# Convolution of batch 1 on 64-by-32 tiles, with its shifted copies made by GpSimd and inside SBUF, batch 2's loads moved behind them, and W2 of group 3 a slot sooner

## The chip, the cores and the metric

One core of a Trainium2 chip. The time is device time of one execution in microseconds (us). A program on one core has no second core to compare clocks with, so each run is listed with the clock that TensorE (PE) was granted. PE does matmuls; VectorE (DVE) and ScalarE (ACT) take results out of PSUM (the kernel's pool there has eight buffers); GpSimd (POOL) makes copies in SBUF and issues the loads of x, which cast from float32 to bf16; SyncE (SP) issues stores, transposes by DMA and, in the changed kernel, three copies inside SBUF.

## The reference, cut to what matters

```python
def _attn_ref(x, weight):              # x: 8 x 4224 x 192, weight: 8 heads x 7 taps
    w = softmax(weight)                # per head
    out = einsum('hk,bskhg->bshg', w, x_unf)      # causal convolution of 7 taps along s

def _moe_ref(x, U, V, w_ch1, w_ch2):   # x: the convolution's result y
    h = x.transpose(0, 2, 1) @ U @ V   # rank 32, sums over all of s of one batch
    u = x + h.transpose(0, 2, 1)
    return u + relu(u @ w_ch1) @ w_ch2
```

The sum over s (`tt` below) needs a batch's whole convolution before the first u of that batch. The 264 tiles of 128 rows are worked off as 33 groups of 8: W1 (u times w_ch1), relu, W2 (times w_ch2), store.

## The kernel before: the parts that matter

```python
    def x_part(b, r, s0, s1):               # one of four loads of a batch, cast to bf16
        blk = NB0 * r + s0 - 1
        return nc.gpsimd.dma_start(out=xt[b][HB * r : HB * r + HB, s0:s1, :], in_=...)

    def x_shift(b):                         # the shifted copy of x for 64-by-32 tiles, 6 steps
        xbt[b] = xbs.tile([P, NB1, D], BF16, name="xb_sb")      # one buffer
        ...
        return [same(0, m), same(m, NB0, (NB0, NB1)),           # 128 partitions each
                ahead(0, 0, m), ahead(0, m, NB0), ahead(1, 0, m), ahead(1, m, NB1)]  # 32 each

    def conv32(b, h0, nh, engs): ...        # 64-by-32 tiles, 8 matmuls a head, needs xbt[b]
    def conv(b, h0, nh, rs, engs, ...): ... # 64-by-64 tiles, 8 matmuls a head, needs only xt[b]

    # a slot: W1 of some groups; W2 of some groups in blocks; what is done ahead of which block
    SLOTS = [
        ([0], [], {}),
        ([1], [0], {0: ["h0"], 1: ["h3", "l2:2"], 2: ["l2:3"]}),           # l: a load
        ([2], [1], {0: ["d1", "h1"], 1: ["t1"], 3: ["s1"], 4: ["h4", "x2:6"]}),
        ([3], [2], {1: ["h5"], 3: ["h6"]}),
        ([4, 5], [3, 4, 5], {0: ["h7"], 2: ["c2:0:3:AAD"], ..., 4: ["c2:6:2:A", "x3:4"], ...}),
    ]
    # d: conv of a batch, and the transpose of group 3 held back until it is over
    # c: conv32; x2:6: six steps of x_shift(2); t, s: sum over s; h: u of a group, then transpose

    # loads of batch b, held until matmuls of W1 of (group, m) are done; each pops one open x_shift step
    LOADS = {2: [(1, 5), (1, 5)], 3: [(4, 1), (4, 4), (5, 1), (5, 4)]}
    for b in range(4, B):
        g = 3 * b - 6
        LOADS[b] = [(g, 0), (g, 3), (g + 1, 0), (g + 1, 3)]
```

## Time and profile before

| kernel before | |
|---|---|
| median (6 runs, lowest to highest) | 325.21 us (325.11 to 325.31) |
| span of the profiled run, granted clock | 323.5 us, 1.0 |
| PE, DVE, ACT, POOL busy | 98%, 83%, 53%, 44% |
| batch 2's loads: first issue, last landing | 29.4, 44.9 us |
| batch 3's loads: first issue, last landing | 60.0, 73.1 us |
| batch 3's convolution starts | 95.1 us |

Four lines of GpSimd's timeline (start, length, engine, line, operation, and in brackets the idle time before it with its releaser):

```profile
42.52 5.43 POOL L293 COPY xb_sb<-x_sb 128x3072 bf16<-128x3072 bf16 x2 [8.89 <-DMA x_sb<-in_x_dram]
...
59.98 1.63 POOL L79 DMA_DIRECT2D x_sb<-in_x_dram  x2
...
71.39 5.43 POOL L293 COPY xb_sb<-x_sb 128x3072 bf16<-128x3072 bf16 x2 [6.20 <-PE ps L339]
...
87.52 3.08 POOL L305 COPY xb_sb<-x_sb 32x3456 bf16<-32x3456 bf16 x1
```

GpSimd alternates: the copies of batch 2 wait for its loads (42.5), the loads of batch 3 are issued only when those copies are over (60.0), and the copies of batch 3 wait for PE's convolution of batch 2 (71.4), because the shifted copy has one buffer. So in the kernel before the loads of batch 3 are there in time, though with only 1.0 us to spare (the last landed at 73.1, its copy began at 74.1), and PE is the releaser. The copies are over at 90.6, 4.5 us before PE wants them.

### The profile page before, as it was taken

What the parts mean: (1) busy time and instruction counts of PE and PEld (TensorE: products, weight loads), DVE (VectorE), ACT (ScalarE), POOL (GpSimd) and SP (SyncE); (2) the same over time, 40 slices, a digit from 0 to 9 for tenths busy, and PEclk for the clock granted to TensorE, in tenths of its full rate; (3) what the DMA queues carried; (4) which work ended last, traced back from release to release, by engine and by line L of the source; (5) the groups of instructions that cost most, each with busy time, mean ns of one, the idle gap of its engine ahead of it and who ended that gap; (6) DMA issues with size and microseconds to landing.
All of it is one profiled execution on the core that took longest, in us unless ns stands there. A gap on an engine that the chain in (4) does not pass through costs nothing.

```text
span 323.5 us, 9584 instructions
## 1 busy us (share of the span) xinstructions
PE 317.1 (98%) x3996; PEld 223.2 (69%) x3996; DVE 269.1 (83%) x551; ACT 170.4 (53%) x344; POOL 142.7 (44%) x111
## 2 busy tenths in 40 slices
PE   6999999999999999999999999999999999999996
PEld 3757676478677647866864784587797497487495
DVE  6769989987977986998798699879898897896864
ACT  1766624860874397088339708824903902912920
POOL 8664179729947694786859497000000000000000
PEclk9999999999999999999999999999999999999999
DMA  8999993999996899699699976139269059048035
GB/s 104 192 192 178 209 211 99 203 195 248 210 153 180 229 175 169 170 162 195 166 238 183 192 162 181 33 112 244 58 168 267 8 149 268 25 121 271 2 119 176
DMA packets 122907, 53.52 MB, mean 165 GB/s; under 512 B 87760, under 2 KB 122832, under 8 KB 122864
## 3 DMA queue, kind: packets, MB, share of 16 engines
q1 hardware_dynamic: 84528, 38.08, 47.0%
q0 software_dynamic: 38192, 14.73, 39.6%
q8 instruction: 31, 0.51, 0.7%
q14 instruction: 12, 0.10, 0.1%
q10 hardware_dynamic: 144, 0.10, 0.1%
HBM read 29.49 MB, written 25.95 MB: 171 GB/s over the span
## 4 chain that ended last, share of the span: by engine, by line
PE 92%; ACT 3%; DMA 2%; DVE 1%; issue 0%; POOL 0%; POOLq 0%
PE ps L583 42%; PE ps L554 39%; PE ps L339 3%; PE ps L457 3%; DMA x_sb<-in_x_dram 2%; PE ps L402 2%; ACT rl_sb L568 2%; PE ps L369 1%; ACT y_sb L256 1%; PE ps L509 1%; DVE u_sb L479 1%; DVE rl_sb L570 1%; PE ps L524 0%; PE ps L428 0%; POOL x_sb L79 0%
## 5 line engine op out<-in xcount | busy, mean ns | idle before, releaser
L568 ACT ACTIVATE rl_sb<-ps 128x512 bf16<-128x512 f32 x233 | 124.3, 603 | 108.0 <-PE ps L554 96.0
L583 PE MATMUL ps<-W_sb,rl_sb 128*128 128x192 bf16 x1584 | 141.9, 246 | 0.2
L583 PEld LDWEIGHTS <-rl_sb 128*128 128x128 bf16 x1584 | 128.1, 98 | 13.5 <-issue 13.1
L554 PE MATMUL ps<-uT,W_sb 64*128 64x512 bf16 x1188 | 131.7, 376 | 0.0
L570 DVE TENSOR_SCALAR rl_sb<-ps 128x512 bf16<-128x512 f32 x163 | 105.3, 688 | 15.7 <-PE ps L554 15.4
L554 PEld LDWEIGHTS <-W_sb 64*128 64x128 bf16 x1188 | 66.9, 94 | 60.5 <-issue 3.9
L592 DVE TENSOR_TENSOR out_sb<-ps,u_sb 128x384 f32<-128x384 f32 (+1 forms) x133 | 70.4, 550 | 25.9 <-PE ps L583 25.4
L305 POOL COPY xb_sb<-x_sb 32x3072 bf16<-32x3072 bf16 (+1 forms) x24 | 67.6, 2826 | 0.7
L479 DVE TENSOR_TENSOR u_sb<-y_sb,ps 128x192 bf16<-128x192 bf16 (+1 forms) x168 | 66.3, 461 | 0.0
L293 POOL COPY xb_sb<-x_sb 128x3072 bf16<-128x3072 bf16 x12 | 32.6, 2744 | 34.6 <-PE ps L339 25.7
L256 ACT ACTIVATE y_sb<-ps 128x384 bf16<-128x384 f32 (+4 forms) x90 | 38.2, 514 | 10.7 <-PE ps L339 7.9
L79 POOL DMA_DIRECT2D x_sb<-in_x_dram x32 | 27.1, 849 | 17.5 <-PE ps L554 10.5
L258 DVE CAST y_sb<-ps 128x408 bf16<-128x408 f32 (+4 forms) x36 | 19.2, 578 | 1.1 <-PE ps L369 0.9
L457 PE MATMUL ps<-tt_sb,V_sb 32*128 32x192 bf16 x264 | 12.4, 246 | 0.1
L339 PE MATMUL ps<-xb_sb,band 64*32 64x384 bf16 x192 | 12.1, 332 | 0.0
L339 PE MATMUL ps<-x_sb,band 64*32 64x384 bf16 x192 | 12.1, 333 | 0.0
L457 PEld LDWEIGHTS <-V_sb 32*128 32x128 bf16 x264 | 4.7, 92 | 7.3 <-issue 7.3
L416 ACT ACTIVATE tt_hi<-ps 128x192 bf16<-128x192 f32 x8 | 2.6, 331 | 10.9 <-PE ps L402 10.9
L369 PE MATMUL ps<-x_sb,band 64*64 64x240 bf16 (+3 forms) x192 | 8.1, 276 | 0.3 <-DMA x_sb<-in_x_dram 0.3
L369 PEld LDWEIGHTS <-band 64*64 64x64 bf16 x192 | 6.0, 106 | 2.2 <-issue 1.5
L339 PEld LDWEIGHTS <-band 64*32 64x32 bf16 x384 | 4.5, 89 | 4.1 <-issue 3.0
L402 PE MATMUL ps<-y_sb,U_sb 128*32 128x192 bf16 x258 | 7.4, 247 | 0.0
(65 smaller groups left out, 69.0 us busy)
## 6 DMA issues: line engine op xcount, KB each, us to landing
out_dram<-out_sb SPq DMA_DIRECT2D x131, 192.0 KB, 2.7
x_sb<-in_x_dram POOLq DMA_DIRECT2D x14, 384.0 KB, 7.3
x_sb<-in_x_dram POOLq DMA_DIRECT2D x7, 432.0 KB, 7.3
x_sb<-in_x_dram POOLq DMA_DIRECT2D x7, 408.0 KB, 8.0
x_sb<-in_x_dram POOLq DMA_DIRECT2D x1, 504.0 KB, 7.6
uT<-u_sb SPq DMA_TRANSPOSE x31, 3.9
x_sb<-in_x_dram POOLq DMA_DIRECT2D x1, 480.0 KB, 5.9
W_sb<-in_moe_w_ch_dram POOLq DMA_DIRECT2D x2, 192.0 KB, 7.6
```

Source lines behind the costliest of these rows:

```text
L79: return nc.gpsimd.dma_start(out=xt[b][HB * r : HB * r + HB, s0:s1, :], in_=x[b, blk * HB : (blk + s1 - s0) * HB, :].rearrange("(j p) d -> ...
L256: nc.scalar.activation(out=out, in_=in_, func=ACT.Copy)
L293: nc.gpsimd.tensor_copy(out=xbt[b][:, s0:s1, :], in_=xt[b][:, s0 + 1 : s1 + 1, :])
L305: nc.gpsimd.tensor_copy(out=xbt[b][q, s0:s1, :], in_=xt[b][q, s0:s1, :])
L339: nc.tensor.matmul(out=pp[r][QB * cg : QB * cg + QB, 0 : nk[r] * GS], lhsT=w[hr], rhs=t[hr, st : st + 2 * nk[r] - 1 : 2, hs], start=True, ...
L457: nc.tensor.matmul(out=banks[pr][:, a * D : (a + 1) * D], lhsT=V_sb[32 * q : 32 * q + 32, (j // 8) * 2 + j % 2, :], rhs=ttb[b][32 * q : 32 ...
L479: nc.vector.tensor_tensor(out=u_group(g)[:, i : i + n, :, hf, :], in0=yt[b][:, run[0] : run[0] + n, :].rearrange("p n (c k) -> p n c k", c=3),
L554: last = nc.tensor.matmul(out=pps[m][hf][:], lhsT=W1_sb[HB * hf : HB * hf + HB, c, m * P : (m + 1) * P], rhs=uTt[g][HB * hf : HB * hf + HB ...
L568: nc.scalar.activation(out=rl[:, m, hf, :], in_=pp[hf][:], func=ACT.Relu)
L570: nc.vector.tensor_scalar_max(out=rl[:, m, hf, :], in0=pp[hf][:], scalar1=0.0)
L583: last = nc.tensor.matmul(out=cps[:, a * D : (a + 1) * D], lhsT=rlt[g][:, m, hf, (i + a) * P : (i + a + 1) * P], rhs=W2_sb[:, m, :], start ...
L592: nc.vector.tensor_tensor(out=o[:, 0:n, :].rearrange("p n (c k) -> p n c k", c=3), in0=cps[:, 0 : n * D].rearrange("p (n c k) -> p n c k", ...
```

## The change

Its intent: batch 1 is convolved with eight tiles at once in place of four, as batches 2 to 7 are. That needs the shifted copy of batch 1, made by three GpSimd steps and three copies inside SBUF. Batch 2's loads move behind GpSimd's steps. W2 of group 3 moves ahead of W1 of groups 4 and 5 and fills the slot in which batch 1's sum is formed.

```diff
+    def x_ahead(b, r, n):
+        q = slice(HB * r + QB, HB * r + HB)
+        s0, s1 = ((0, NB0 // 2), (NB0 // 2, (NB0, NB1)[r]))[n]
+        nc.sync.dma_start(out=xbt[b][q, s0:s1, :], in_=xt[b][q, s0:s1, :])
@@ slots
-        ([0], [], {}),
-        ([1], [0], {0: ["h0"], 1: ["h3", "l2:2"], 2: ["l2:3"]}),
-        ([2], [1], {0: ["d1", "h1"], 1: ["t1"], 3: ["s1"], 4: ["h4", "x2:6"]}),
-        ([3], [2], {1: ["h5"], 3: ["h6"]}),
+        ([0], [], {0: ["X", "w0:0", "w1:0"]}),
+        ([1], [0], {0: ["h0"], 1: ["h3"], 2: ["w0:1"]}),
+        ([2], [1], {0: ["h1"], 2: ["c1:0:3:AAD"], 3: ["c1:3:3:AAD"], 4: ["c1:6:2:AD", "x2:6"]}),
+        ([3], [2, 3], {0: ["t1"], 1: ["s1"], 2: ["h4"], 5: ["h5"]}),
         (
             [4, 5],
-            [3, 4, 5],
+            [4, 5],
    ... (h, t, s and the heads of batches 2 and 3 in new places of their slots)
-    LOADS = {2: [(1, 5), (1, 5)], 3: [(4, 1), (4, 4), (5, 1), (5, 4)]}
+    LOADS = {3: [(4, 1), (4, 4), (5, 1), (5, 4)]}
@@ what a slot can ask for
+        if what == "X":
+            st = x_shift(1)
+            for n in (0, 1, 5):
+                st[n]()
+            x_tile(2)
+            x_zero(2, nc.gpsimd)
+            for q in (0, 2, 1, 3):
+                x_part(2, *XP[q])
+            return
```

The transpose of group 3 is no longer held back either (`if n > 1 and n != 3` became `if n > 1`).

More of the change, by code (lines that the diff above doesn't have):

```diff
@@ L619 @@
     SLOTS = [
-        ([0], [], {}),
-        ([1], [0], {0: ["h0"], 1: ["h3", "l2:2"], 2: ["l2:3"]}),
-        ([2], [1], {0: ["d1", "h1"], 1: ["t1"], 3: ["s1"], 4: ["h4", "x2:6"]}),
-        ([3], [2], {1: ["h5"], 3: ["h6"]}),
+        ([0], [], {0: ["X", "w0:0", "w1:0"]}),
+        ([1], [0], {0: ["h0"], 1: ["h3"], 2: ["w0:1"]}),
+        (
+            [2],
+            [1],
+            {
+                0: ["h1"],
+                2: ["c1:0:3:AAD"],
+                3: ["c1:3:3:AAD"],
+                4: ["c1:6:2:AD", "x2:6"],
+            },
+        ),
+        ([3], [2, 3], {0: ["t1"], 1: ["s1"], 2: ["h4"], 5: ["h5"]}),
         (
             [4, 5],
-            [3, 4, 5],
+            [4, 5],
             {
-                0: ["h7"],
-                2: ["c2:0:3:AAD"],
-                3: ["c2:3:3:AAD"],
-                4: ["c2:6:2:A", "x3:4"],
+                0: ["h6"],
+                2: ["c2:0:2:A"],
+                3: ["c2:2:3:AAD"],
+                4: ["c2:5:3:AAD", "x3:4"],
+                5: ["h7"],
                 6: ["t2"],
-                8: ["s2"],
-                9: ["h8"],
-                11: ["h9"],
+                7: ["s2"],
+                8: ["h8"],
             },
@@ L638 @@
     ]
-    nh = 10
+    nh = 9
     for k in range(5, 14):
         gs = list(range(3 * k - 9, 3 * k - 6))
-        hs = [f"h{g}" for g in range(nh, min(nh + 3, NG))] + [None] * 3
-        nh = min(nh + 3, NG)
+        hs = [f"h{g}" for g in range(nh, min(nh + 4, NG))] + [None] * 3
+        nh = min(nh + (4 if k == 5 else 3), NG)
         if k == 5:
             at = {
-                2: ["c3:0:3:AAD"],
-                3: ["c3:3:3:AAD"],
-                4: ["c3:6:2:A", "x4:3"],
-                5: [hs[0]],
+                0: [hs[0]],
+                2: ["c3:0:2:A"],
+                3: ["c3:2:3:AAD"],
+                4: ["c3:5:3:AAD", "x4:3"],
+                5: [hs[1]],
                 6: ["t3"],
-                8: ["s3", hs[1]],
-                11: [hs[2]],
+                8: ["s3", hs[2]],
+                11: [hs[3]],
             }
@@ L768, in do @@
             return
-        if what[0] == "d":
-            for h in range(H):
-                last = conv(int(what[1:]), h, 1, [0, 1], "AA" if h == 2 else "AD")
-            held(transp(3), last)
+        if what == "X":
[6 more added lines that the diff above has]
+                x_part(2, *XP[q])
             return
-        if what[0] == "l":
-            b, q = (int(v) for v in what[1:].split(":"))
-            x_load(b, q, done_w2[-1])
+        if what[0] == "w":
+            x_ahead(1, *(int(v) for v in what[1:].split(":")))
             return
@@ L786, in do @@
             h_group(n)
-            if n > 1 and n != 3:
+            if n > 1:
                 transp(n)
```

## The prediction

> **What bounds the kernel now.** I read the page first, then the chain that ended last in order of time, then the timeline from 20 to 102 us, stage by stage. The page says that TensorE (PE) carries almost everything:
>
> ```profile
> PE 317.1 (98%) x3996; PEld 223.2 (69%) x3996; DVE 269.1 (83%) x551; ACT 170.4 (53%) x344; POOL 142.7 (44%) x111
> PE 92%; ACT 3%; DMA 2%; DVE 1%; issue 0%; POOL 0%; POOLq 0%
> ```
>
> The first line is busy time by engine, the second the chain by engine. From about 68 us on the chain is PE alone, one matmul group after another, so only two things move the end: less PE work, or fewer stalls of PE before 68 us. These are the chain's pieces (start, length, what) where batch 1 is convolved:
>
> ```profile
> 33.92 2.09 PE ps L554 x18
> 36.02 2.54 ACT rl_sb L568 x5
> 38.56 3.10 ACT y_sb L256 x8
> 41.65 0.04 issue
> 41.70 1.15 PE ps L583 x12
> ```
>
> The chain leaves PE for 5.6 us, which looks like a large prize. It is not a PE gap of 5.6 us. The timeline of the same stretch (start, length, engine, line, operation) shows PE nearly always occupied there:
>
> ```profile
> 33.85 4.06 PE L554 MATMUL ps<-uT,W_sb 64*128 64x512 bf16 x36
> 37.84 3.24 PE L369 MATMUL ps<-x_sb,band 64*64 64x384 bf16 x64
> 38.44 3.59 ACT L256 ACTIVATE y_sb<-ps 128x384 bf16<-128x384 f32 x9
> 38.59 3.51 DVE L258 CAST y_sb<-ps 128x408 bf16<-128x408 f32 x7
> 41.02 0.63 PE L457 MATMUL ps<-tt_sb,V_sb 32*128 32x192 bf16 x8
> 47.22 3.10 PE L554 MATMUL ps<-uT,W_sb 64*128 64x512 bf16 x25
> 56.42 8.24 PE L554 MATMUL ps<-uT,W_sb 64*128 64x512 bf16 x72
> ```
>
> Batch 1's convolution is the 64 matmuls of L369, paced by 16 evictions on ACT (9 in 3.59 us) and VectorE (DVE, 7 in 3.51 us), since eight PSUM banks are all there are. So the honest measure is a budget of PE time.
>
> From the start of W1 of group 2 (33.85) to that of group 6 (81.17, L554 x108 in the timeline) before takes 47.3 us. Its work at undisturbed rates: four W1 groups at 3.92 (108 in 11.76 us later in the chain, over 3) = 15.7; 20 W2 blocks, most 1.10 alone or 2.09 a pair, about 1.05 = 21.0; batch 1's conv at 64-by-64, about 2.64 (64 x 396 columns at the row time that W1 shows, 3.92 us / 18 pairs = 0.218 us per 512 columns, four tiles at once: 16 x 0.168 = 2.7); batch 2's conv 1.82 (0.64 + 0.71 + 0.47, batch 3's three bursts); two tt sums of 0.85 and 0.17 = 2.0; seven h groups at 0.3 = 2.1. Sum 45.3. **Stalls: about 2.0 us**, of which I can name 0.5 in the conv (3.24 against 2.7), 0.3 in the h group after it (0.63 against 0.34), 0.5 in W1 of group 3 (47.22 to 51.61 is 4.4), 0.4 in W1 of groups 4 and 5 (8.24 against 7.84).
>
> **What the Trainium skill says.** "TensorEngine Tiling (Array Packing)", Available Configurations, lists four tiles for 64x64 and eight for 64x32; its PSUM Bottleneck says that tiling speeds up TensorE but not the evacuation of PSUM. The trace agrees with both: 64 matmuls take 1.82 us as 64-by-32 in batch 3 and 3.24 as 64-by-64 in batch 1, and the latter are paced by evictions. "SBUF — State Buffer", SBUF: two separate sides, says that VectorE and GpSimd share a port pair that is locked when GpSimd works beside a VectorE operation with two SBUF inputs. The add that makes u has one input in SBUF and one in PSUM, and four of them take 1.94 us both at 29.73, with GpSimd issuing loads only, and at 42.02, beside a copy; so I charge nothing for new copies beside DVE. "DMA: Bandwidth & Descriptors", Anatomy of one DMA, fits 2.0 us plus bytes over 436 GB/s (for the GpSimd path): 2.45 us for the 192 KB of one SBUF copy. In the trace 192 KB stores land in 2.7 us at the median, but in 4.7 in the first 80 us; I use 2.7 to 4.7.
>
> **The change part by part.**
> *Removed on PE:* 64 matmuls at 64-by-64 (2.7 undisturbed). *Added:* 64 at 64-by-32 in bursts of 3, 3 and 2 heads between W2 blocks (1.82). Sum -0.9 us of work. The number of evictions stays 16, but they now have W2 blocks beside them, so PE shouldn't be paced by them: most of the 0.8 in conv and h goes too. ACT takes 10, DVE 6; one DVE eviction less is 0.5 us on an engine that is busy over 94% from 25 to 70 us.
> *Added on GpSimd:* two copies of 128 partitions (2.74 each), one small (0.50), one of 3.07. The last parts of batch 1's x are issued at 21.24 and 22.1 and land after 7.3 and 9.1 us, at 28.5 and 31.2. So the copies run 28.5-31.3, 31.3-34.0, 34.0-34.5, 34.5-37.6. They lie beside W1 and W2 of groups 0 to 2; the conv now comes after W1 of group 2, one h group and two W2 blocks: 33.85 + 3.92 + 0.4 + 2.1, near 40.4. Hidden by some 2.8 us.
> *Added on the Sync queue:* three copies in SBUF. The last stands behind the transpose of group 3 (its u is done at 34.0; 1.4 to 1.7 us of issue) and a store, so it is issued near 36.2 and lands at 39 to 41. That is when PE gets there: I charge 0 to 0.6, 0.2 expected.
> *Moved:* all loads of batch 2 go from 29.4-33.6 to 37.7-41.2, landing at 45 to 50. Its six GpSimd steps (before: 42.52 to 59.8) then run about 46.5 to 64. Its conv starts after W1 of 4 and 5, near 70. Hidden by 6 us.
> *W2 of group 3 a slot sooner:* no work added or removed. It fills PE between h4/h5 and W1 of 4 and 5, and DVE can catch up (before, W1 of 4 began with 2 us of adds and a store outstanding on DVE, first relu at 58.59). Its cost is that h4 comes later against W1 of 4. By the queue: conv ends near 44.6, W1 of group 3 to 48.7, tt sum 49.6, W2, s1 50.9, W2, h4 at 52.2; DVE adds until 54.6 (six in 2.06), transpose lands 4 to 4.7 later, 58.6 to 59.3; PE reaches W1 of 4 after six more W2 blocks and h5, near 59. So 0 to 0.7 of wait, 0.3 expected; the same for group 5, whose adds end near 58.4, landing near 63, against 63.
> *GpSimd for batch 3:* from the end of batch 2's conv, the chain of six copies and two loads took 71.3 to 90.6 = 19.2 us; the conv of batch 3 started 23.8 us after it. With four W2 blocks fewer in that slot (4.3) this becomes 19.5. Slack falls from 4.6 to 0.3 us: expected wait 0.1.
> *Sum:* -0.9 work. Stalls: 2.0 now; after it 0.2 (SBUF copy) + 0.4 (uT of 4, 5) + 0.1 (batch 3) + 0.7 (W1 of 2 to 5 still paced by evictions) = 1.4, so -0.6. Together -1.5. I shade it to **-1.3 us: 324.0 us**, as three hand-overs are within half a microsecond of being late.
>
> **The rivals.**
> *1. A new wait eats the gain.* The Sync copy, the transpose of group 4 or the last GpSimd copy of batch 3 comes 1 to 2 us late. For it: the hand-overs above; stores of 18 to 36 us took 6.6 us to land, and at that the last copy lands at 42.8. Against it: those stores met batch 2's loads, which are gone from there. Time 325 to 327.
> *2. The whole 5.6 us of the chain is won* by removing the convolution that it passes through. For it: the chain names ACT there. Against it: PE's timeline is full. It would give 319.7; I hold it at 2%.
> *3. DVE is the bound up to 70 us,* and one eviction fewer with the same other work gives only 0.5: 324.8. For it: DVE over 94% busy there. Against it: PE's work alone fills 45.3 of the 47.3 us, so DVE can cost at most those 2.
>
> **Range and chances.** Best case: no stall but 0.6, -2.3, 323.0. Bad case: rival 1 with one late hand-over, +0.4, 325.7. I give 322.7 to 325.7. 2% is 6.5 us, over twice what work and stalls together offer, and slower by 6.5 needs a late load of some 8 us. So faster 0.01, same 0.97, slower 0.02.
>
> **What would show it.** Batch 1's 64 matmuls under the 64-by-32 line in three bursts of 0.6, 0.7 and 0.5 us; the first between 40 and 41.5. No GpSimd copy of batch 1 ending after 38.5. W1 of group 6 starting at 79.4 to 80, against 80.9 (81.17 less the 0.3 of an h group that moved behind it). PE idle or waiting ahead of W1 of 4 or 5 for a transpose, under 0.7. The prediction is wrong if PE waits over 1 us for a DMA or GpSimd at a conv, or if the stalls of W1 do not shrink and only the 0.9 is seen.

## More of the kernel before

The profile counts the packets of all DMA queues on one set of 16 DMA engines (before: 47.0% of their time for the queue of stores and transposes, 39.6% for that of GpSimd's loads).

In the timelines shown here GpSimd's steps start in the order in which the program issues them. The pool of x has two buffers, the shifted copy one, the results waiting for their store eight.

## The result, and the profile after

| | before | after |
|---|---|---|
| median (6 runs each) | 325.21 us | 341.82 us (339.83 to 342.3) |
| ratio | | 1.0502 (95%: 1.0476 to 1.0528) |
| granted clock | 1.0 | 0.973 to 0.99 |

The change costs 5%, 16.6 us. A ratio is the mean time of one kernel's fast runs over that of the other's of the same rounds, so not quite the ratio of the medians.

The page's busy line and its chain by engine, as the prediction showed them of before:

```profile
PE 320.9 (94%) x3996; PEld 220.9 (65%) x3996; DVE 268.7 (79%) x550; ACT 171.5 (50%) x345; POOL 151.8 (45%) x115
PE 67%; POOL 11%; DMA 10%; issue 0%; DVE 0%; POOLq 0%
```

POOL and DMA carry a fifth of the span in a chain that was PE's. Two rows of the page's 40 slices (8.5 us each, busy tenths of PE and granted clock) show where:

```profile
PE   7999999999195999999999999999999999999995
...
PEclk9999999999587799999999999999999999999999
```

One stretch is hurt, around slices 11 to 14 (85 to 119 us); all else is as full as before. PE's timeline (with W1 under L560 and the 64-by-32 convolution under L345):

```profile
34.15 4.06 PE L560 MATMUL ps<-uT,W_sb 64*128 64x512 bf16 x36
...
59.35 2.98 PE L560 MATMUL ps<-uT,W_sb 64*128 64x512 bf16 x26 [0.79 <-DMA uT<-u_sb]
...
79.91 4.34 PE L560 MATMUL ps<-uT,W_sb 64*128 64x512 bf16 x36
91.94 10.32 PE L560 MATMUL ps<-uT,W_sb 64*128 64x512 bf16 x72 [7.69 <-DMA uT<-u_sb]
...
108.42 0.50 PE L345 MATMUL ps<-xb_sb,band 64*32 64x408 bf16 x1 [3.53 <-POOL xb_sb L305]
```

Up to 79.91 us PE does what was intended: W1 of group 6 starts 1.0 us sooner than it would have before (80.9 with the h group that moved; counted from W1 of group 2, which began 0.3 us later in this run, it is 1.3 us less). Then it waits 7.7 us for a transpose, and at 104.6 to 108.4 for GpSimd's copy of batch 3. The second wait is the one that sets the end. This is the chain in order of time (start, length, what), from the loads of batch 2 to that convolution:

```profile
38.36 2.40 POOL x_sb L79 x3
40.76 14.39 DMA x_sb<-in_x_dram
...
55.20 2.74 POOL xb_sb L293
...
58.55 5.43 POOL xb_sb L305 x2
...
64.04 5.77 POOL xb_sb L305 x2
...
70.03 2.40 POOL x_sb L79 x3
72.43 19.28 DMA x_sb<-in_x_dram
...
91.83 2.74 POOL xb_sb L293
...
95.18 5.44 POOL xb_sb L305 x2
...
108.42 0.88 PE ps L345 x11
```

Load batch 2, copy batch 2, load batch 3, copy batch 3: but for one copy of each batch (at 49.4 and 88.1 us), which ran while the last load was still under way, each step waits for the one before. Beside the kernel before:

| us | before | predicted | after | after - before |
|---|---|---|---|---|
| batch 2: first load issued | 29.4 | 37.7 | 38.3 | 8.9 |
| batch 2: last load landed | 44.9 | 50 | 55.2 | 10.2 |
| batch 2: copies over | 59.8 | 64 | 69.8 | 10.0 |
| batch 3: first load issued | 60.0 | not worked out | 70.0 | 10.0 |
| batch 3: last load landed | 73.1 | not worked out | 91.7 | 18.6 |
| batch 3: copies over | 90.6 | 19.2 after batch 2's conv | 108.4 | 17.8 |
| batch 3: conv can run on | 95.1 | 19.5 after batch 2's conv | 108.4 | 13.3 |

The landings are issue plus the time that the trace gives for each load: for batch 3 before 6.1, 7.3, 8.0, 8.8 us; after 7.2, 11.2, 16.4, 19.3 us. The four land one after another (2.1 to 2.7 us apart before, 3.7 to 6.0 after), so the time of the last holds its wait for the other three. The 17.8 us of lateness use up the slack of 4.5 us and 13.3 remain. From there to batch 4's convolution it is 27.3 us before (95.1 to 122.4) and 29.7 after (108.4 to 138.1), and that is the clock: PE had idled, and was granted half. Of four stretches (time, then busy us and instruction count by engine; the third number from the end is the granted clock):

```profile
88.00:92.00 4.00, 0.06 (x2) 0.07 (x4) 0.00 (x0) 0.00 (x0) 2.91 (x2) 0.50 1.30 232
92.00:97.00 5.00, 5.00 (x26) 1.84 (x28) 1.38 (x2) 2.20 (x4) 4.90 (x3) 0.52 0.52 119
97.00:102.00 5.00, 5.00 (x50) 2.14 (x46) 4.24 (x7) 4.71 (x10) 4.83 (x5) 1.00 0.00 0
...
108.00:114.00 6.00, 5.58 (x62) 3.65 (x62) 1.60 (x3) 3.36 (x8) 2.02 (x3) 0.51 1.36 213
```

The same W1 matmuls go at 26 in 5 us at a clock of 0.52 and at 50 in 5 us at 1.0; two W2 blocks after 108.4 take 2.0 and 1.8 us in place of 1.1. The Trainium skill, "TensorE: Matmul & The Clock Gate", What's actually happening, says that the array idles at half its clock until it has been busy for a while; the trace agrees (0.50 to 0.52). So 13.3 + 2.4 = 15.7 of the 16.3 us of span are placed. The last 0.6 lies behind the kernel's last add: from its end to the end of the span it is 3.4 us in place of 2.8. This tail is between 2.6 and 4.4 us in the profiles of this case, and what sets it was not traced; it matters for the small differences below.

### The profile page after: what moved, and what is told of

Read it like the earlier page. It is cut to its first block, busy times and chain, and to the rows that moved or that the text cites. A ratio compares the mean times of both kernels' runs of the same rounds, so it can differ in the third digit from the quotient of the medians.

```text
span 339.8 us, 9600 instructions
## 1 busy us (share of the span) xinstructions
PE 320.9 (94%) x3996; PEld 220.9 (65%) x3996; DVE 268.7 (79%) x550; ACT 171.5 (50%) x345; POOL 151.8 (45%) x115
## 3 DMA queue, kind: packets, MB, share of 16 engines
q0 software_dynamic: 38192, 14.73, 38.5%
## 4 chain that ended last, share of the span: by engine, by line
PE 67%; POOL 11%; DMA 10%; issue 0%; DVE 0%; POOLq 0%
PE ps L589 33%; PE ps L560 28%; DMA x_sb<-in_x_dram 10%; POOL xb_sb L305 7%; PE ps L345 3%; PE ps L463 2%; POOL x_sb L79 2%; POOL xb_sb L293 2%; PE ps L408 1%; POOL xb_sb L295 0%; PE ps L434 0%; DVE out_sb L598 0%; POOL x_sb L74 0%; POOLq L74 0%; POOLq L293 0%
## 5 line engine op out<-in xcount | busy, mean ns | idle before, releaser
L589 PE MATMUL ps<-W_sb,rl_sb 128*128 128x192 bf16 x1584 | 143.5, 248 | 0.1
L560 PE MATMUL ps<-uT,W_sb 64*128 64x512 bf16 x1188 | 133.8, 381 | 8.5 <-DMA uT<-u_sb 8.5
L560 PEld LDWEIGHTS <-W_sb 64*128 64x128 bf16 x1188 | 64.5, 95 | 73.7 <-DMA uT<-u_sb 9.2
L598 DVE TENSOR_TENSOR out_sb<-ps,u_sb 128x384 f32<-128x384 f32 (+1 forms) x133 | 70.1, 550 | 28.8 <-PE ps L589 28.5
L305 POOL COPY xb_sb<-x_sb 32x3072 bf16<-32x3072 bf16 (+1 forms) x25 | 70.6, 2836 | 0.7
L293 POOL COPY xb_sb<-x_sb 128x3072 bf16<-128x3072 bf16 x14 | 38.1, 2744 | 49.4 <-DMA x_sb<-in_x_dram 22.1
L256 ACT ACTIVATE y_sb<-ps 128x408 bf16<-128x408 f32 (+4 forms) x91 | 38.7, 509 | 19.4 <-PE ps L345 16.4
L345 PE MATMUL ps<-xb_sb,band 64*32 64x384 bf16 x224 | 15.2, 348 | 3.5 <-POOL xb_sb L305 3.5
L345 PE MATMUL ps<-x_sb,band 64*32 64x384 bf16 x224 | 14.8, 350 | 0.0
L345 PEld LDWEIGHTS <-band 64*32 64x32 bf16 x448 | 5.5, 91 | 8.6 <-issue 7.2
L153 PE MATMUL ps<-zz 128*128 128x512 f32 (+1 forms) x10 | 6.1, 754 | 1.1 <-DVE zz L143 1.1
L408 PEld LDWEIGHTS <-U_sb 128*32 128x32 bf16 x258 | 5.4, 96 | 1.7 <-issue 1.4
```

Of the source, the lines that this page charges most:

```text
L256: nc.scalar.activation(out=out, in_=in_, func=ACT.Copy)
L293: nc.gpsimd.tensor_copy(out=xbt[b][:, s0:s1, :], in_=xt[b][:, s0 + 1 : s1 + 1, :])
L305: nc.gpsimd.tensor_copy(out=xbt[b][q, s0:s1, :], in_=xt[b][q, s0:s1, :])
L345: nc.tensor.matmul(out=pp[r][QB * cg : QB * cg + QB, 0 : nk[r] * GS], lhsT=w[hr], rhs=t[hr, st : st + 2 * nk[r] - 1 : 2, hs], start=True, ...
L560: last = nc.tensor.matmul(out=pps[m][hf][:], lhsT=W1_sb[HB * hf : HB * hf + HB, c, m * P : (m + 1) * P], rhs=uTt[g][HB * hf : HB * hf + HB ...
L589: last = nc.tensor.matmul(out=cps[:, a * D : (a + 1) * D], lhsT=rlt[g][:, m, hf, (i + a) * P : (i + a + 1) * P], rhs=W2_sb[:, m, :], start ...
```

## The experiments

Two theories stood at the start. **The serial chain**: batch 2's loads come late because they stand behind GpSimd's copies of batch 1, and GpSimd's order hands that on to batch 3. **Contention**: the DMA engines are shared, and the loads are slow because they meet stores, transposes and copies. Others were the W2 move, and the new copies and convolution themselves. All medians below are beside the kernel before on the same chip, 325.2 to 325.4 us.

### 1. Batch 2's loads between GpSimd's copies of batch 1

```diff
-            for n in (0, 1, 5):
-                st[n]()
-            ... all four loads of batch 2
+            st[0]()
+            ... loads 0 and 2
+            st[1]()
+            ... loads 1 and 3
+            st[5]()
```

> The changed kernel, with the four loads of batch 2 issued between GpSimd's copies of batch 1 (two after the first copy, two after the second) in place of behind them all; nothing else differs. Serial-chain theory (loads of batch 2 behind batch 1's copies, batch 2's copies behind the loads, loads of batch 3 behind those copies, batch 3's copies last): batch 2 is issued near 32 and 36 us in place of 38 to 42, its last load lands before 48 (55.2 now), its copies end near 62 (69.8 now), batch 3 is issued near 62 and lands before 76 (91.7 now), its copies end near 94, and the time falls to 324 to 327. Contention theory (the DMA engines are simply too full with stores, transposes and loads whatever their order): loads still take 14 us and more, time above 335.

Measured: 337.17 us, ratio 1.0364. Batch 2 was issued at 31.4 and 36.4 us as planned, but its last load took 17.3 us and landed at 54.5. The new thing is in the chain:

```profile
40.01 9.99 DMA xb_sb<-x_sb
```

The last copy inside SBUF now stood behind those loads and landed 10.0 us after issue (3.0 at the median for the three in the changed kernel), and PE waited 9.7 us for it at batch 1's convolution. The serial chain's numbers missed. Contention's came true (over 14 us, above 335), but by another path: 9.7 of the 12.0 us lost are that one wait, and batch 3's loads, issued at 74.0, took only 5.1 to 8.1 us each (the last landed at 86.7). So this run decides between neither; it shows that the loads hurt a small transfer that batch 1 still waits for.

### 2. W2 of group 3 put back

```diff
-        ([3], [2, 3], {0: ["t1"], 1: ["s1"], 2: ["h4"], 5: ["h5"]}),
+        ([3], [2], {0: ["t1"], 1: ["s1"], 2: ["h4"], 3: ["h5"]}),
-            [4, 5],          # W2 of the next slot
+            [3, 4, 5],
```

> The changed kernel with W2 of group 3 put back behind W1 of groups 4 and 5; the rest as changed. Theory that the shortened slot took GpSimd's slack for batch 3: 4.3 us of PE work come back between the convolutions of batches 2 and 3, so time falls by about 4, to 337 to 338. Serial-chain theory: GpSimd and the loads set the start of batch 3's convolution at about 108 us whatever PE does before, so the time stays within 1.5 us of 341.8.

Measured: 342.5 us (341.31 to 345.65), ratio 1.0558; the median is within 1 us of the changed kernel's. Where W2 of group 3 stands did not matter while loads and GpSimd set the time.

### 3. The W2 move alone, on the kernel before

```diff
-        ([3], [2], {1: ["h5"], 3: ["h6"]}),
+        ([3], [2, 3], {1: ["h5"], 3: ["h6"]}),
-            [3, 4, 5],
+            [4, 5],          # and t2, s2, h8, h9 ahead of blocks 5, 6, 7, 8
```

> The kernel before with one part alone: W2 of group 3 moved ahead of W1 of groups 4 and 5, batch 1's convolution and all loads as before. Every theory that blames loads or copies of batches 1 and 2: within 1 us of 325.2. If the W2 move by itself costs (it leaves GpSimd 4.3 us less between the convolutions of batches 2 and 3): 326 to 329.

Measured: 327.4 us, ratio 1.0066. It costs 2.2 us by itself in this form, but only 1.0 of it is in the work: the last add ends at 321.7 us in place of 320.7, and the tail behind it is 4.0 us in place of 2.8. W1 of groups 6 to 8 took 13.0 us (81.1 to 94.1) in place of 11.9, with the adds of h9 on DVE ahead of the relus; how much of that is the move and how much the new places of h8 and h9 was not separated.

### 4. Batch 3's loads between batch 2's copies

```diff
-                4: ["c1:6:2:AD", "x2:6"],
+                4: ["c1:6:2:AD", "x2:1"],
-    LOADS = {3: [(4, 1), (4, 4), (5, 1), (5, 4)]}
+    LOADS = {3: [(3, 1), (3, 2), (3, 3), (3, 4)]}
```

> The changed kernel with only the second link cut: the loads of batch 3 are issued between batch 2's copies (from W1 of group 3 on, as soon as batch 1's buffer is free) and no longer behind them; batch 2's loads stay behind batch 1's copies. Serial-chain theory: batch 2's last load still lands at 54 to 57, batch 3's loads land before 78 in place of 91.7, batch 3's convolution starts near 95, time 324 to 328. If the late batch 2 alone were the cause: no better than 337.

Measured: 332.09 us, ratio 1.0206 (330.28 to 333.22). With batch 2 just as late (last landing 56.3), batch 3 landed at 75.6 and 9.7 us came back. So the second link, loads of batch 3 behind copies of batch 2, carries most of the loss. The range of 324 to 328 was missed: batch 3's convolution started at 101.2 us, not near 95. Batch 3's loads now ran beside the transposes of groups 4 and 5, for which PE waited 1.7 and 2.6 us, and in this run the last SBUF copy of batch 1 was issued just behind batch 2's first load and cost 1.3 us more. From the waits of this run (in all, times, longest):

```profile
PE ps L560 <- DMA uT<-u_sb: 4.3, 2, 2.6
```

### 5. The changed kernel without the stores of groups 0 to 5

```diff
-        eng.dma_start(out=out_t[:, t : t + n, :], in_=o[:, 0:n, :])
+        if g > 5:
+            eng.dma_start(out=out_t[:, t : t + n, :], in_=o[:, 0:n, :])
```

> The changed kernel with the stores of groups 0 to 5 left out (the result is wrong there on purpose); everything else as changed. If the loads of batches 2 and 3 are slow because they share the DMA engines with the stores: last load of batch 2 lands within 10 us of issue (14.4 now), of batch 3 within 10 us (19.3 now), time 324 to 329. If the loads are slow by themselves or by their issue order: within 3 us of 341.8.

Measured: 330.94 us, ratio 1.0186. Its output is wrong, which doesn't matter for the time. Two lines of its chain:

```profile
40.49 10.08 DMA x_sb<-in_x_dram
...
67.83 13.65 DMA x_sb<-in_x_dram
```

Without stores the last loads of batches 2 and 3 take 10.1 and 13.7 us from issue in place of 14.4 and 19.3, and 10.9 of the 16.6 us are gone. So most of the loss needs the stores; the kernel before was not run without them, so what leaving them out saves by itself is not known. The time and batch 3's load missed their marks (324 to 329, 10 us), for the chain is still loads and GpSimd's copies, up to batch 4's convolution at 127.8 us (122.4 before). Late loads do not catch up by themselves.

### 6. Late loads alone, on the kernel before

Nothing of the change but the time at which batch 2 is loaded:

```diff
-        ([1], [0], {0: ["h0"], 1: ["h3", "l2:2"], 2: ["l2:3"]}),
+        ([1], [0], {0: ["h0"], 1: ["h3"]}),
-    LOADS = {2: [(1, 5), (1, 5)], 3: ...
+    LOADS = {2: [(2, 5)] * 4, 3: ...
```

> The kernel before (64-by-64 convolution, no shifted copies of batch 1, W2 where it was) with one thing changed: the four loads of batch 2 are held until W1 of group 2 is nearly through, so that they are issued near 37 to 41 us as in the changed kernel (29.4 to 33.6 in the kernel before). Theory that the late issue of batch 2's loads is the cause: last load of batch 2 lands near 51 to 55, its copies end near 67 to 70, batch 3's loads are issued near 67 to 70 and land in 12 us and more, time 333 to 342. Theory that the new GpSimd copies, SBUF copies or the new convolution cost it: no more than 328.

Measured: 334.07 us, ratio 1.0266. The copies of batch 2 end at 70.1 us (69.8 in the changed kernel). But the chain names another wait:

```profile
40.98 12.63 DMA uT<-u_sb
```

This kernel holds the transpose of group 3 back until batch 1's convolution is over, so here it was issued behind the late loads, and PE waited 6.5 us for it.

### 7. The same with that transpose let go first

```diff
-                last = conv(int(what[1:]), h, 1, [0, 1], "AA" if h == 2 else "AD")
-            held(transp(3), last)
+                conv(int(what[1:]), h, 1, [0, 1], "AA" if h == 2 else "AD")
-            if n > 1 and n != 3:
+            if n > 1:
```

> The kernel before with batch 2's loads issued near 38 to 41 us (as in the run before of that kind, 334.1 us) and the transpose of group 3 no longer held back until batch 1's convolution, so that it is out before the loads, as in the changed kernel. In the run with it held, TensorE lost 6.5 us waiting for that transpose behind the loads, and came so late to W1 of groups 4 and 5 that batch 3's loads ran beside it. Theory that late loads of batch 2 alone make the whole loss of the changed kernel: TensorE is early again, batch 3's loads (issued near 70) meet the stores of W2, land 16 us and more after issue, its convolution starts at 102 to 108 and the time is 334 to 341. Theory that the late loads cost only through that transpose: 325 to 328.

Measured: 339.91 us, ratio 1.0423 (1.0349 to 1.0498). GpSimd's timeline, and the wait that ends it on PE (L339 is the 64-by-32 convolution in this numbering):

```profile
66.92 3.37 POOL L79 DMA_DIRECT2D x_sb<-in_x_dram  x4
85.50 2.74 POOL L293 COPY xb_sb<-x_sb 128x3072 bf16<-128x3072 bf16 x1 [15.21 <-DMA x_sb<-in_x_dram]
...
107.50 0.50 PE L339 MATMUL ps<-xb_sb,band 64*32 64x408 bf16 x1 [7.43 <-POOL xb_sb L305]
```

This is the changed kernel's loss without its convolution, its copies of batch 1 or its W2 move: batch 3's last load takes 21.4 us, its convolution runs on at 107.5 us (108.4 there), and 14.7 of the 16.6 us are there. **Late loads of batch 2 are enough to make most of the loss.** (The interval is wide because one run of the kernel before took 329.19 us; the kernel before with nothing but this transpose let go was not run.) That they cost more here than with the transpose held fits the phase: there PE came late itself, and batch 3's last load took 13.3 us in place of 21.4.

### 8. Batch 1's last GpSimd copy by DMA too, ahead of the loads

```diff
-            for n in (0, 1, 5):
+            for n in (0, 1):
... the w steps in new places of their slots
-        nc.sync.dma_start(out=xbt[b][q, s0:s1, :], in_=xt[b][q, s0:s1, :])
+        nc.scalar.dma_start(out=xbt[b][q, s0:s1, :], in_=xt[b][q, s0:s1, :])
```

> The changed kernel with the last GpSimd copy of batch 1 also made by a copy inside SBUF, all four of these issued from ScalarE's queue before the batch 2 loads can be in their way, and batch 2's loads behind two GpSimd copies in place of three (issued near 35 to 39 in place of 38 to 42). If the issue time of batch 2 is what counts, each us sooner gives about one: 336 to 339, unless the four SBUF copies land after 41.5 and hold up the convolution, which would give 340 and more.

Measured: 341.26 us, ratio 1.0496. The last of the four copies was issued at 34.8 us, together with the first load, and landed after 8.9; batch 1's convolution waited until 43.8. Three us won at the issue of batch 2 did not help: its loads took up to 19.6 us, and its second GpSimd copy began at 57.0 us, later than in the changed kernel (55.2).

### 9. The 64-by-64 convolution cut in two

```diff
-        ([2], [1], {0: ["d1", "h1"], 1: ["t1"], 3: ["s1"], ...
+        ([2], [1], {0: ["d1:0:4", "h1"], 1: ["d1:4:4"], 2: ["t1"], 3: ["s1"], ...
```

> The kernel before with batch 1's 64-by-64 convolution cut in two halves of four heads with a W2 block between them, and nothing else. My budget said that 0.5 to 0.8 us of PE time is lost there to evictions that have no other PE work beside them: 324.4 to 324.9. If nothing is lost there (PE is full): 325.2 or a little more.

Measured: 326.47 us, ratio 1.0033 (1.0021 to 1.0046). Slower by 1.1 us, where I had expected a gain of 0.5. But the split is not what costs it: the last add ends at 320.8 us, as before (320.7), and the tail behind it is 4.1 us in place of 2.8. From W1 of group 2 to W1 of group 6 it took 47.7 us in place of 47.3, so the gain is missing, and no more. (The edit also moved t1 one block back.) The chain of this run leaves PE for DVE from 36.4 to 44.2 us (relus, evictions, adds and one store's add, one after the other):

```profile
36.45 1.99 DVE rl_sb L570 x3
38.44 1.39 DVE y_sb L258 x3
...
42.64 1.56 DVE y_sb L258 x3
...
81.38 11.84 PE ps L554 x108
```

So in this run DVE's queue paces that stretch, and other PE work beside the evictions did not help.

### 10. Batch 3's loads beside W1

```diff
-                4: ["c1:6:2:AD", "x2:6"],
+                4: ["c1:6:2:AD", "x2:2"],
-    LOADS = {3: [(4, 1), (4, 4), (5, 1), (5, 4)]}
+    LOADS = {3: [(4, 0), (4, 0), (4, 0), (4, 0)]}
```

> The changed kernel with batch 3's four loads put between the last four GpSimd copies of batch 2, from the start of W1 of group 4 on, so that they are issued near 60 to 70 us, most of them beside W1 of groups 4 and 5, which stores nothing. GpSimd's copies of batch 2 end 4 us later (near 74), which delays batch 2's convolution. If batch 3's lateness is one of issue behind the copies and of meeting the stores: its loads land before 79, its convolution starts at 97 to 100, time 328 to 331. If batch 3's loads are slow wherever they are: no better than 337.

Measured: 333.22 us, ratio 1.0233 (1.0162 to 1.0304). The loads took 7.7, 6.2, 7.9 and 9.3 us, where the changed kernel's took 7.2 to 19.3. So batch 3's loads are not slow by nature. They were also issued 3.5 us apart, and the last two ran beside W2; place and spacing were not separated. The time missed 328 to 331, and the last load landed at 80.6, not before 79. The remaining loss has moved to batch 2's convolution, which waited 5.0 us for its copies, as these were delayed by the loads between them.

### 11. Only batch 3's loads later, on the kernel before

```diff
-    LOADS = {2: [(1, 5), (1, 5)], 3: [(4, 1), (4, 4), (5, 1), (5, 4)]}
+    LOADS = {2: [(1, 5), (1, 5)], 3: [(5, 5)] * 4}
```

> The kernel before with only batch 3's four loads held until the end of W1 of group 5 (issued near 65 to 68 us in place of 60 to 64.3), so that they run beside W2 and its stores and no longer beside W1, which stores nothing; nothing of batch 2 changes. In the kernel before the copies of batch 3 end 4.5 us before its convolution needs them. If only the issue time counts: loads land near 77, the slack takes it, 325 to 326.5. If loads that meet the stores are stretched, as in the changed kernel: last landing 82 to 88, time 328 to 333.

Measured: 331.48 us, ratio 1.0192. Issued at 64.9 to 67.4 us, the last load took 14.8 us and landed at 82.2. The number was expected, its path was not: the copies ended at 98.8 us, and PE itself only came to batch 3's convolution at 100.3. The chain goes through a store that took 10.6 us to land (the median of the whole run before is 2.7); all eight result buffers were waiting for their stores, and DVE stood still for 4.5 us. The store from the chain, and the wait from DVE's timeline:

```profile
70.84 10.61 DMA out_dram<-out_sb
...
81.57 0.56 DVE L592 TENSOR_TENSOR out_sb<-ps,u_sb 128x384 f32<-128x384 f32 x1 [4.48 <-DMA out_dram<-out_sb]
```

So the meeting hurts both sides.

Together: neither theory is enough alone. GpSimd's order hands the lateness on (runs 4, 6, 7), and the meeting with stores and transposes makes it larger (runs 5, 11). None of the eleven was faster than the kernel before, which stays the best version.

## Why the prediction was wrong

324.0 us (322.7 to 325.7) was predicted and 341.8 measured.

**Right, up to 80 us.** The first burst of batch 1's convolution was to start at 40 to 41.5: 40.50. No GpSimd copy of batch 1 past 38.5: 38.13. The last SBUF copy was to land at 39 to 41: issued at 36.6, 3.2 us, 39.7. The wait ahead of W1 of group 4 was to be under 0.7: 0.79, a touch over. W1 of group 6 at 79.4 to 80: 79.91. The charge of nothing for GpSimd's copies beside DVE held too: four u adds took 1.94 us beside a copy at 30.0.

**The step that failed** is "GpSimd for batch 3: from the end of batch 2's conv, the chain of six copies and two loads took 71.3 to 90.6 = 19.2 us", with "Slack falls from 4.6 to 0.3 us: expected wait 0.1". I took over the releaser of the kernel before, PE's convolution of batch 2, and never worked out when batch 3's data would be there. The trace had batch 3's loads there only 1.0 us before their copies. Now they were issued behind batch 2's copies at 70.0 and landed at 91.7 us. From the end of batch 2's convolution (73.9) to the end of the copies it took not 19.2 but 34.5 us: PE waited 3.5 us at that convolution, where the prediction called 1 us a sign of being wrong, after 7.7 us for a transpose beside the same loads, and ran on 13.3 us later than before. My working had the copies of batch 2 ending at 64; one step further would have put batch 3's loads on top of the W2 blocks of groups 4 and 5.

**A mis-sized term ahead of it:** "landing at 45 to 50". I gave batch 2's loads 7 to 9 us each; four issued within 3 us took 7.6, 10.0, 13.2 and 14.4, so the last landed at 55.2 and batch 2's copies were over at 69.8, not 64. The trace before already had 11.4 and 12.2 us for the last two of these same loads, beside the stores of group 0. "Hidden by 6 us" was hidden by none: PE came to that convolution at 69.8, so that it, and W1 of group 6 behind it, were still on time was luck. Run 5, without stores, had 10.1 us in place of 14.4.

**Rival 1 had the mechanism and not the size.** It foresaw "a new wait eats the gain" and a late last GpSimd copy of batch 3, "1 to 2 us late". It also said of stores and loads that "those stores met batch 2's loads, which are gone from there"; the loads were not gone but had moved to meet the next stores. And the sentence that a loss of 6.5 us "needs a late load of some 8 us" was true: batch 3's last load came 18.6 us late.

**The budget of stalls held in its sum, not shown in its reason.** From W1 of group 2 to that of group 6 PE took 1.3 us less, as forecast; so rival 2, which wanted 5.6, is out. I blamed evictions without PE work beside them, but run 9 gives them such work and gains nothing. There DVE paces the stretch from 36 to 44 us, which speaks for rival 3; for the kernel before that was not tested.

**What stays open.** From first issue to last landing the four loads of batch 3 took 13.2 us in the kernel before, 16.1 without stores (run 5), 21.7 in the changed kernel. Batch 2's four in run 5, issued at once with neither store nor transpose in flight, took 12.5. So issuing them at once cost nothing; about 3.6 us (16.1 less 12.5) came with the transposes and 5.6 with the stores, each from a single profile. What sets the tail behind the last add, and with it over half of run 3's 2.2 us, was not traced.

## What to carry to other kernels

When an issue moves later, follow its data to the next thing that the same queue does, and on from there for two turns of the loop: here 8.9 us at batch 2 became 17.8 at batch 3, because loads and copies shared GpSimd's order, the slack (1.0 us at the loads, 4.5 at the convolution) was small, and the late loads met stores that stretched them. The releaser that a profile names holds for that profile's order only; ask of each input anew when it arrives. And place bulk loads where the kernel stores nothing and needs no small transfer: mostly beside W1 the four landed 2.1 to 2.7 us apart (before), beside W2's stores 3.7 to 6.0 (after), and they stretched transposes, SBUF copies and stores alike. Last, look where a difference of 1 us lies before explaining it: in run 9 it was in the tail, far from the edit.

## What the Trainium skill lacked or had wrong

- "DMA: Bandwidth & Descriptors", Issuing engines are not separate DMA queues, says that DMAs from scalar, sync and gpsimd run on the same 16 engines and interleave. The runs agree, and give what the page lacks, a size: the 192 KB copies inside SBUF took 2.9 to 3.2 us with the loads of batch 2 not yet issued, 8.9 and 10.0 beside them (runs 8 and 1); a transpose 12.6 us (run 6); a store 10.6 (run 11).
- The same page, Anatomy of one DMA, fits 2.0 us plus bytes over 436 GB/s per DMA on GpSimd's path. For the 408 KB load that makes 3.0 us (an estimate from the page; the trace shows this load written in pieces of 384 bytes, for which the fit may not be meant); the trace has 8.8 in the quiet stretch before and 19.3 after, both behind three other loads; a 384 KB load with no other ahead of it took 5.2 (after, issued at 100.9; 2.9 by the same estimate). No section sizes casting loads that are issued together: four of them (1.6 MB landed) took 12.5 us at best here (run 5).
- No page that I read says that loads can hold up stores until the result buffers run out, which then looks like a slow DVE (4.5 us in run 11).
